# Two attention blocks on one core: V loads ahead of a K wave that has an x transfer behind it, and the second batch's x transposed one step later

## The chip, the core and the metric

The kernel runs on one core of a Trainium2 chip. Its time is the device time of one execution in microseconds, and the median over a few executions is compared. A profile is one more execution, recorded by the hardware profiler; its own time is given beside it. The core has a matrix engine (TensorE, "PE" in the profile, with its weight loads as "PEld"), three engines for elementwise work (VectorE "DVE", ScalarE "ACT", GpSimd "POOL"), a sequencer that issues most DMA transfers (SyncE, "SP") and 16 DMA engines that carry them out. TensorE writes to PSUM banks; the other engines copy from there to SBUF.

## What is computed

Two attention blocks of the same shape (A and B) run after each other, and their outputs stand side by side. For each of 16 batches and 16 heads, with 144 queries, 512 cached keys and a head size of 256:

```python
q = (x @ wq).reshape(B, Sq, H, Dh).transpose(0, 2, 1, 3)
scores = jnp.einsum("bhqd,bhkd->bhqk", q, k_cache) * (Dh ** -0.5)
p = softmax(scores, axis=-1)
o = jnp.einsum("bhqk,bhkd->bhqd", p, v_cache)
return o.transpose(0, 2, 1, 3).reshape(B, Sq, H * Dh) @ wo
```

x is 16 x 144 x 448, the caches are 16 x 16 x 512 x 256, wq is 448 x 4096 and wo 4096 x 448, all in bfloat16. The caches are most of what has to be read.

## The kernel before

**Units and steps.** A unit is one head of one batch of one block; there are NT = 512 of them. The program is a long list of steps i from -4 (`s_min = -LT`) on, and in step i it does, for TensorE in this order: a transpose of K for unit i+4 (only for the first P0 = 48 units, `t_tr`), the query projection of a later unit (`t_q`, "Q", three or four units ahead; from the 49th unit on mostly two batches in one, so that some steps have none), the scores of unit i+2 or i+3 (`t_s`, "S"), the product with V of unit i (`t_pv`, "PV"), the row sums (`t_sum`) and pieces of the output projection (`t_op_piece`). The exponentials and the logarithm are on ScalarE, most copies out of PSUM on VectorE, the partial row sums on GpSimd. A scheduler records every instruction with what it reads and writes and puts in the waits. Each engine runs its list in order, so an instruction that waits holds up everything behind it on its engine.

**Loads.** All big loads go through SyncE's queue, in one order:
- V: `t_load_v(G)` brings V for the two units 2G and 2G+1 (512 KB) into one of NV = 9 slots of `v_sb`. It is needed at PV of unit 2G. In this text v181 is the load for units 362 and 363.
- K: the first 48 units' K is loaded as it lies (`t_load_n`, "n", into the same slots) and transposed by TensorE. After that a K wave, `t_load_k(W)`, brings 16 units (two first waves 8) by one DMA transpose into `kt_sb`, which holds KR = 32 units. A wave overwrites what the wave before the last brought, so it has to wait for the last S on that. k21 is the wave for units 368 to 383.
- x: batches 0 and 1 of block A are loaded as they lie (`t_load_xn`) and transposed by TensorE in the steps that X_AT names (`t_tr_x`, L1018, with copies at L1024 on VectorE and L1028 on ScalarE). The other batches come in groups (X_GROUPS, mostly four batches) by DMA transposes (`t_load_x`, L982 to L990) into NX = 6 places. x6 is the group with batches 24 to 27 (8 to 11 of block B).
- wq and wo by plain loads in groups (`t_load_wq`, `t_load_wo`); the first two heads' wq go through ScalarE's queue.

**The planner.** The order of the loads is worked out when the program is built. `clock` sums assumed durations of TensorE work for each step, and `at(i)` is when step i begins by it. Each load has a due time (`at` of its first use, minus MARGIN = 1.0), a step from which its place is free, and an assumed duration: 1.44 for a V, 2.0+0.55 for each batch of an x group, 2.4+0.97 for each unit of a K wave. `slip` is how far the plan has fallen behind so far. From these the loop takes one load after the other. Among loads that can start now it takes the one with the smallest latest start (due time plus slip minus duration). Between a K wave and another load the rule is another one: the K wave goes first if the other's latest start is later than the wave's duration plus HOLD from now:

```python
if k_new == k_old:
    better = latest < best[1]
elif k_new:
    better = best[1] > start + m[2] + HOLD
else:
    better = latest <= start + best[2][2] + HOLD
```

Right after a K wave an x group that can start goes first, and counts 1.4 less. The first four loads are fixed by the list `first` (x of batch 0, two halves of K, x of batch 1). `dma_plan` is then issued in this order; each load's semaphores make SyncE wait until its place is free.

**The start.** Before the first data arrive TensorE runs WARM = 34 matmuls on ones (L930). Step -4 transposes x of batch 0, step -3 x of batch 1 and then does Q of unit 0 (batch 0), step -2 does Q of unit 1 (batch 1).

Of the kernel before, what the change touches and what calls it, by code (L numbers as in the profile page):

```python
# [752 lines left out]
def bass_concat_heads__mha_block_cached__gqa_block_cached__near_ridge_kernel(  # L753
# [45 lines left out]
    X_GROUPS = ((2, 6), (6, 10), (10, 14), (14, 18), (18, 20), (20, 24), (24, 28), (28, 32))  # L799
    assert X_GROUPS[-1][1] == NP * Bn and H == KW  # L800
    WQ_GROUPS = ((2, 4), (4, 8), (8, 12), (12, 16))
    WARM = 34
    NQT, NPT, NPS, NRI, NOST = 11, 4, 2, 2, 2
    RS = 3
    RC = RS * 128
    XR, X_AT = 48, {0: -4, 1: -3}
    OP_DELAY, OP_START, OP_RATE = 2, (28, 16), ((240, 1.0), (292, 1.35), (600, 1.15))
    MARGIN, HOLD, K_FIX = 1.0, 1.0, 2.4
    NXGT = len(X_GROUPS)

    P0 = NNAT * UV
# [11 lines left out]
    with contextlib.ExitStack() as es:  # L823
# [79 lines left out]
        def t_init():  # L903
# [23 lines left out]
            def e6(t):  # L927
                ins = None
                for _ in range(WARM):
                    ins = t.matmul(op_ps[:, 0:128], lhsT=ones[:, :], rhs=ones[:, :], start=True, stop=True)  # L930
# [439 lines left out]
        s_min = -LT  # L1370
# [59 lines left out]
        def at(i):  # L1430
            return clock[max(i, s_min)]
# [14 lines left out]
        def load_list():  # L1446
            made = []

            def load(use, free, took, fn, *args):
                made.append((at(use) - MARGIN, free, took, fn, args))  # L1450

            for XG, (g0, g1) in enumerate(X_GROUPS):
                load(first_q[g0], (g1 - NX) * H - lq(NT) if g1 > NX else s_min, 2.0 + 0.55 * (g1 - g0), t_load_x, XG)
            for W, (u0, u1) in enumerate(WAVES):
                last = u1 - 1 - KR
                load(u0 - ls(u0), last - ls(last) + 1 if last >= 0 else s_min, K_FIX + 0.97 * (u1 - u0), t_load_k, W)
            for pr in range(NP):
                for h0, h1 in WQ_GROUPS if pr == 0 else [(h, h + 4) for h in range(0, H, 4)]:
                    load(first_h[pr, h0], NU - H + h1 - lq(NU) if pr else s_min, 0.78 * (h1 - h0), t_load_wq, pr, h0, h1)
                for wg in range(NWG):  # L1460
                    load(wo_use[pr, wg], wo_done[pr - 1, wg] + 1 if pr else s_min, 1.3, t_load_wo, pr, wg)
            for g in X_AT:
                load(X_AT[g], s_min, 0.4, t_load_xn, g)
            for u in range(4):
                load(u - LT, s_min, 0.72, t_load_n, u // 2, u % 2)
            for G in range(2, NNAT):
                load(UV * G - LT, None, 1.44, t_load_n, G)
            for G in range(NT // UV):
                load(UV * G, None, 1.44, t_load_v, G)
            return made  # L1470

        todo = sorted(load_list(), key=lambda m: m[0])
        dma_plan, due, ring_free, now, slip = [], [], [], 2.0, 0.0
# [3 lines left out]
        while todo:  # L1477
            n = len(ring_free)
            v_lo = ring_free[n - NV] if n >= NV else s_min
            best = None  # L1480
            after_k = len(dma_plan) and dma_plan[-1][0] is t_load_k
            for m in todo[:60]:
                lo = v_lo if m[1] is None else m[1]
                start = max(now, at(lo) + slip if lo > s_min else now)
                latest = m[0] + slip - m[2]
                if len(first) and m[3:] == first[0]:
                    best = (start, -1e9, m, lo)
                    break
                if after_k and m[3] is t_load_x and start <= now:
                    best = (start, latest, m, lo)  # L1490
                    break
                if best is None or max(start, now) < max(best[0], now):
                    best = (start, latest, m, lo)
                elif max(start, now) == max(best[0], now):
                    k_new, k_old = m[3] is t_load_k, best[2][3] is t_load_k
                    if k_new == k_old:
                        better = latest < best[1]
                    elif k_new:
                        better = best[1] > start + m[2] + HOLD
                    else:  # L1500
                        better = latest <= start + best[2][2] + HOLD
                    if better:
                        best = (start, latest, m, lo)
            if first:
                first.pop(0)
            now, _latest, m, lo = best
            now += m[2] - (1.4 if after_k and m[3] in (t_load_k, t_load_x) else 0.0)
            slip = max(slip, now - m[0])
            todo.remove(m)
            dma_plan.append(m[3:])  # L1510
            due.append(lo)
            if m[1] is None:
                v_seq["n" if m[3] is t_load_n else "v", m[4][0]] = len(ring_free)
                ring_free.append(UV * (m[4][0] + 1) - (LT if m[3] is t_load_n else 0))
# [141 lines left out]
```

## Time and profile before

| | us |
|---|---|
| median of 4 runs | 1053.46 |
| lowest and highest | 1051.64, 1055.43 |
| profiled execution: its time | 1055.05 |
| profiled execution: span from first to last instruction | 1053.3 |
| TensorE waits over 1 us with work of the kernel behind them | 4.0 (V), 3.1 (V), 2.0 (K wave), 1.4 (x of batch 1) |
| K wave by DMA transpose, median from issue to landing | 24.1 (A), 24.9 (B) |
| V load, median from issue to landing | 7.2 (A), 7.6 (B) |

The profile's page gives the busy time of each engine, the waits of an engine give who was waited for (total, times, longest), a timeline gives start, duration, engine, line and operation in order of time, with a wait in brackets. "SPq" rows are DMA issues on SyncE; their duration is that of the issue, and the landing of the data is later. The windows view gives for chosen stretches the busy time of each engine, the clock that TensorE was granted (1.00 is full) and the DMA engines' share.

### The profile page before, as it was taken

How to read it: one execution, taken by the hardware profiler on the slowest of the kernel's cores; microseconds unless marked ns; L12 is line 12 of the kernel's file. 1: busy time of each engine (PE TensorE's matmuls, PEld its weight loads, DVE VectorE, ACT ScalarE, POOL GpSimd, SP SyncE). 2: the span in 40 equal slices, each digit the busy share in tenths (PEclk: the TensorE clock that was granted, in tenths of full speed). 3: DMA queues.
4: the chain of work that ended last, by engine and by line, in shares of the span. 5: the costliest groups of instructions: out<-in, count | busy, mean ns of one | idle time of the engine just before them, and what ended most of it. 6: DMA issues, size and time to landing. Idle time of an engine off the chain costs nothing.

```text
span 1053.3 us, 32452 instructions
## 1 busy us (share of the span) xinstructions
PE 1034.5 (98%) x12434; PEld 878.7 (83%) x12434; DVE 740.0 (70%) x2042; ACT 794.1 (75%) x2368; POOL 635.0 (60%) x1030
## 2 busy tenths in 40 slices
PE   9999999999998999999999999999899999999997
PEld 8999888888886888888888788888788888888885
DVE  5776677777665776777776677777576667777775
ACT  6877677777775787777867678787687777788785
POOL 3655556666664666666655566666565656666673
PEclk9999999999999999999999999999999999999999
DMA  9999999999999999999999999999999999999950
GB/s 328 366 333 322 298 260 255 278 279 285 293 281 302 274 253 272 279 291 298 270 295 353 254 282 290 291 285 292 287 283 246 296 251 311 281 272 285 283 200 13
DMA packets 590884, 294.10 MB, mean 279 GB/s; under 512 B 501440, under 2 KB 515904, under 8 KB 590720
## 3 DMA queue, kind: packets, MB, share of 16 engines
q1 hardware_dynamic: 589760, 291.49, 110.9%
q8 instruction: 99, 1.62, 0.6%
q10 hardware_dynamic: 960, 0.46, 0.2%
q14 instruction: 65, 0.53, 0.1%
HBM read 161.74 MB, written 4.13 MB: 157 GB/s over the span
## 4 chain that ended last, share of the span: by engine, by line
PE 93%; DMA 4%; ACT 1%; SPq 1%; DVE 1%; issue 0%; POOL 0%; ACTq 0%; DVEq 0%
PE s_ps L1164 23%; PE ot_ps L1220 23%; PE qp_ps L1133 23%; PE op_ps L1336 19%; DMA kt_sb<-in_B_k_cache_dram 2%; PE ot_ps L1236 2%; PE s_ps L1084 1%; PE qp_ps L1084 1%; PE qp_ps L1336 1%; DMA v_sb<-in_A_v_cache_dram 1%; ACT rinv_sb L1257 0%; DMA wo_sb<-in_A_x_dram 0%; DMA v_sb<-in_B_v_cache_dram 0%; ACT pt_sb L1174 0%; SPq L982 0%
## 5 line engine op out<-in xcount | busy, mean ns | idle before, releaser
L1184 POOL TENSOR_TENSOR pp_sb<-pt_sb 128x288 f32<-128x288 bf16 x512 | 384.2, 750 | 321.7 <-ACT pt_sb L1174 307.1
L1174 ACT ACTIVATE pt_sb<-s_ps 128x288 bf16<-128x288 f32 x1024 | 364.5, 408 | 175.9 <-PE s_ps L1164 169.6
L1272 DVE TENSOR_TENSOR ring<-ot_ps,rinv_sb 128x288 bf16<-128x288 f32 (+2 forms) x640 | 241.6, 394 | 150.9 <-ACT rinv_sb L1257 147.4
L1220 PE MATMUL ot_ps<-pt_sb,v_sb 128*128 128x144 bf16 x4096 | 340.7, 226 | 7.1 <-DMA v_sb<-in_A_v_cache_dram 4.0
L1164 PE MATMUL s_ps<-qt_sb,kt_sb 128*128 128x144 bf16 x4096 | 340.6, 226 | 2.9 <-DMA kt_sb<-in_B_k_cache_dram 2.0
L1164 PEld LDWEIGHTS s_ps<-qt_sb,kt_sb 128*128 128x128 bf16 x4096 | 287.5, 98 | 56.1 <-DVE qt_sb L1147 5.6
L1257 ACT ACTIVATE rinv_sb<-ln_sb 64x144 f32<-64x144 f32 x928 | 298.3, 321 | 24.2
L1133 PE MATMUL qp_ps<-xt_sb,wq_sb 128*128 128x288 bf16 (+1 forms) x2368 | 302.0, 271 | 0.3 <-DVE qt_sb L1146 0.2
L1336 PE MATMUL op_ps<-wo_sb,ring 128*128 128x448 bf16 x1120 | 286.3, 353 | 0.0
L1220 PEld LDWEIGHTS ot_ps<-pt_sb,v_sb 128*128 128x128 bf16 x4096 | 274.5, 98 | 8.3 <-DMA v_sb<-in_A_v_cache_dram 4.2
L1133 PEld LDWEIGHTS qp_ps<-xt_sb,wq_sb 128*128 128x128 bf16 x2368 | 212.0, 98 | 75.2 <-DVE qt_sb L1146 0.9
L1189 POOL TENSOR_TENSOR p_sb<-pp_sb 128x144 f32<-128x144 f32 x464 | 226.7, 489 | 74.7 <-DVE ps_sb L1198 10.1
L1287 DVE TENSOR_REDUCE run_sb<-ot_ps 128x1 bf16<-128x144 f32 x560 | 146.4, 304 | 83.4 <-ACT ln_sb L1244 52.6
L1198 DVE TENSOR_TENSOR ps_sb<-p_sb 64x144 bf16<-64x144 f32 x464 | 158.3, 341 | 45.8 <-POOL p_sb L1189 32.4
L1147 DVE CAST qt_sb<-qp_ps 128x576 bf16<-128x576 f32 x216 | 162.0, 750 | 16.2 <-PE qp_ps L1133 13.9
L1336 PEld LDWEIGHTS op_ps<-wo_sb,ring 128*128 128x128 bf16 x1120 | 93.9, 98 | 20.1
L1244 ACT ACTIVATE ln_sb<-ot_ps 128x144 f32<-128x144 f32 x232 | 67.7, 292 | 40.3 <-PE ot_ps L1236 33.4
L1236 PE MATMUL ot_ps<-ps_sb,ones 128*128 128x144 bf16 x280 | 63.5, 227 | 0.0
L1146 DVE CAST qt_sb<-qp_ps 128x288 bf16<-128x288 f32 x80 | 35.8, 447 | 2.2 <-PE qp_ps L1133 1.8
L1092 ACT ACTIVATE kt_sb<-qp_ps 128x512 bf16<-128x512 bf16 x48 | 29.0, 604 | 1.2 <-PE qp_ps L1084 1.2
L1189 POOL TENSOR_TENSOR ps_sb<-pp_sb 128x144 bf16<-128x144 f32 x48 | 23.4, 488 | 6.9 <-PE ot_ps L1236 0.3
L1236 PEld LDWEIGHTS ot_ps<-ps_sb,ones 128*128 128x128 bf16 x280 | 27.5, 98 | 0.0
(37 smaller groups left out, 163.8 us busy)
## 6 DMA issues: line engine op xcount, KB each, us to landing
v_sb<-in_A_v_cache_dram SPq DMA_DIRECT2D x128, 512.0 KB, 7.2
v_sb<-in_B_v_cache_dram SPq DMA_DIRECT2D x128, 512.0 KB, 7.6
v_sb<-in_A_k_cache_dram SPq DMA_DIRECT2D x22, 512.0 KB, 9.7
out_dram<-ost_sb SPq DMA_DIRECT2D x36, 112.0 KB, 6.3
wo_sb<-in_A_wo_dram SPq DMA_DIRECT2D x8, 448.0 KB, 8.0
wo_sb<-in_B_wo_dram SPq DMA_DIRECT2D x8, 448.0 KB, 8.3
wq_sb<-in_B_wq_dram SPq DMA_DIRECT2D x4, 768.0 KB, 9.7
wq_sb<-in_A_wq_dram SPq DMA_DIRECT2D x3, 768.0 KB, 9.2
```

The source lines that it names most:

```text
L1133: ins = t.matmul(acc, lhsT=wq_sb[:, kc, c0:c0 + 128], rhs=xt_sb[:, kc, xo:xe + 1:max(xe - xo, 1), :], start=(kc == 0), stop=(kc == 3))
L1147: return v.tensor_copy(qt_sb[:, a:b + 1:b - a, :, :], qp_ps[:, :, 0:2 * SQ].rearrange("p e (u q) -> p u e q", u=2))
L1164: ins = t.matmul(s_ps[bank][:, (c % 2) * SQ:(c % 2 + 1) * SQ], lhsT=kt_sb[:, 2 * c + dc, ko:ko + 128], rhs=qt_sb[:, qsl, dc, :], start=(dc ...
L1174: return a.activation(pt_sb[:, psl, 2 * k:2 * k + 2, :].rearrange("p b q -> p (b q)"), s_ps[bank][:, 0:2 * SQ], AF.Exp, scale=DH ** -0.5)
L1184: return g.tensor_tensor(pp_sb[:, :, :], pt_sb[:, psl, 0:2, :], pt_sb[:, psl, 2:4, :], op=ALU.add)
L1189: return g.tensor_tensor(dst, pp_sb[:, 0, :], pp_sb[:, 1, :], op=ALU.add)
L1198: return v.tensor_tensor(ps_sb[p0:p0 + 64, sl, :], p2_sb[0:64, :], p2_sb[64:128, :], op=ALU.add)
L1220: ins = t.matmul(ot_ps[ob][:, dc * SQ:(dc + 1) * SQ], lhsT=v_sb[:, vsl, j, c * DH + dc * 128:c * DH + (dc + 1) * 128], rhs=pt_sb[:, sl, c, ...
L1257: return a.activation(rinv_sb[p0:p0 + 64, sl, :], ln_sb[h0:h0 + 64, :], AF.Exp, scale=-1.0)
L1272: ins = v.tensor_tensor(ring[:, 2 * h:2 * h + 2, r0:r0 + q1 - q0], ot_ps[ob][:, 0:2 * SQ].rearrange("p (c q) -> p c q", c=2)[:, :, q0:q1], ...
L1287: return v.tensor_reduce(run_sb[:, k, j:j + 1], ot_ps[ob][:, 2 * SQ:3 * SQ], axis=AX.X, op=op)
L1336: ins = t.matmul(acc[0:m, 0:D], lhsT=ring[:, c, col0:col0 + m], rhs=wo_sb[:, c, :], start=(c == op_first), stop=(c == op_last))
```

## The change

Three constants and the planner's rule are changed. WARM goes from 34 to 32. X_AT has x of batch 1 transposed in step -2, ahead of that step's K transpose and of Q of unit 1, instead of in step -3. And where the planner weighs a K wave against another load, the bound is raised by the durations of all x groups (times X_HOLD = 1.0) whose place is free at that moment:

```diff
-    WARM = 34
+    WARM = 32
...
-    XR, X_AT = 48, {0: -4, 1: -3}
+    XR, X_AT = 48, {0: -4, 1: -2}
...
-    MARGIN, HOLD, K_FIX = 1.0, 1.0, 2.4
+    MARGIN, HOLD, K_FIX, X_HOLD = 1.0, 1.0, 2.4, 1.0
...
             after_k = len(dma_plan) and dma_plan[-1][0] is t_load_k
+            behind = sum(X_HOLD * m[2] for m in todo[:60] if m[3] is t_load_x and (m[1] == s_min or at(m[1]) + slip <= now))
             for m in todo[:60]:
...
                     elif k_new:
-                        better = best[1] > start + m[2] + HOLD
+                        better = best[1] > start + m[2] + HOLD + behind
                     else:
-                        better = latest <= start + best[2][2] + HOLD
+                        better = latest <= start + best[2][2] + HOLD + behind
```

No load, no compute instruction and no buffer is added or removed apart from the two matmuls on ones; what changes is the order of loads on SyncE's queue and of TensorE's work in steps -3 and -2.

## The prediction

> **What bounds the kernel now.** I read the page's busy shares first, then who TensorE waited for, then the SyncE timeline around the waits, then the granted clock in the windows beside them.
>
> ```profile
> PE 1034.5 (98%) x12434; PEld 878.7 (83%) x12434; DVE 740.0 (70%) x2042; ACT 794.1 (75%) x2368; POOL 635.0 (60%) x1030
> DMA  9999999999999999999999999999999999999950
> ```
>
> TensorE is busy 98% of the span, and the DMA engines are as full. So TensorE sets the end, and what is to be won lies in the few waits that it has:
>
> ```profile
> PE ot_ps L1220 <- DMA v_sb<-in_A_v_cache_dram: 4.0, 1, 4.0
> PE ot_ps L1220 <- DMA v_sb<-in_B_v_cache_dram: 3.1, 1, 3.1
> PE s_ps L1164 <- DMA kt_sb<-in_B_k_cache_dram: 2.0, 1, 2.0
> PE op_ps L1018 <- DMA wo_sb<-in_A_x_dram: 1.4, 1, 1.4
> ```
>
> Two waits for V, one for a K wave, one for the second batch's x at the start. Each is a single event. The SyncE timeline at the second one:
>
> ```profile
> 722.68 1.65 SPq L1054 DMA_DIRECT2D v_sb<-in_B_v_cache_dram  x3
> 725.77 22.39 SPq L1040 DMA_TRANSPOSE kt_sb<-in_B_k_cache_dram  x1
> 748.20 3.33 SPq L982 DMA_TRANSPOSE xt_sb<-in_B_x_dram  x1
> 751.58 2.63 SPq L1054 DMA_DIRECT2D v_sb<-in_B_v_cache_dram  x5
> ```
>
> The last V before the wave is v180, the wave is k21 (wave 21), then x6, then v181. v181 landed at 755.40 (3.8 after its issue), and PV of unit 362 waited for it until 755.53. After a long wait the clock is lost too:
>
> ```profile
> 4.10:7.51 3.41, 1.97 (x40) 1.61 (x37) 0.75 (x2) 0.77 (x2) 0.00 (x0) 1.00 1.07 307
> 7.51:10.93 3.42, 3.42 (x33) 3.34 (x33) 1.69 (x4) 0.88 (x2) 0.00 (x0) 0.50 1.05 382
> 598.01:601.43 3.42, 2.44 (x27) 1.72 (x24) 2.20 (x7) 1.64 (x5) 1.32 (x3) 1.00 1.29 257
> 601.43:604.84 3.41, 2.43 (x28) 2.08 (x29) 0.63 (x2) 1.35 (x4) 1.05 (x2) 1.00 1.16 272
> 751.62:755.03 3.41, 0.81 (x11) 0.57 (x9) 1.43 (x3) 0.80 (x3) 1.96 (x4) 1.00 1.14 300
> 755.03:758.45 3.42, 2.92 (x21) 2.50 (x22) 1.05 (x4) 1.34 (x4) 0.00 (x0) 0.50 1.04 362
> ```
>
> The second column is the stretch's length, the third PE's busy time, the third from the end the granted clock. A stretch with 1.44 us idle (1.97 busy) is followed by one at half clock, one with 0.98 idle (2.44 busy) is not.
>
> **The start: WARM and X_AT.** WARM drops two matmuls of 3.50/34 = 0.10 us each. That is 0.2 us if nothing covered it; it is covered, since the next PE work waits for loads whose issue doesn't move: 0. X_AT adds and removes nothing: 12 transposes, a 0.38 us DVE copy and a 0.28 us ACT copy go behind the rest of step -3 (TR of unit 1, Q of unit 0). The x load keeps its place, because the list `first` fixes it, and no queue is passed. PE then does TR1 and Q0 while the x is on its way (landed 6.95), so the 1.4 us wait and the half-clock stretch behind it go. I place TX1 at 7.08 as before, TR2 at 7.9 (its K half, issued 2.81, landed 5.0 later), Q1 at 8.45 (behind the x copies, now directly ahead of it), TR3 at 9.7 instead of 11.58: 1.9 earlier. But this runs into loads that don't move. v1 landed at 16.8 (issue 6.75 plus 10.1) and PV2 would be there at 18.50-1.9 = 16.6. The second wq group landed at 22.7 (issue 9.07 plus 13.6); Q of unit 8, which needs it, ran at 23.30 and can't be ahead of 22.8. Of 1.9 us at most 0.5 stays. The new wait before Q8 is about 1.1 us, between 0.98 (no half clock) and 1.44 (half clock, half of 3.41 us = 1.7 lost). So the start is worth -0.5 to +1.2; I take -0.3.
>
> By the Trainium skill (TensorE: Matmul & The Clock Gate, section on the HAM clock gate) the array goes back to half rate only after at least one idle window of some 3.4 us. The trace differs: 1.44 us idle inside 3.41 was enough. By the page no new wait of 1 to 2 us would have a clock price, and the upper ends here would be 1.2 to 1.7 lower; the rows decide.
>
> **The planner.** Its numbers only order loads; they are no times of the chip. Each load has a latest start: due time plus slip minus its duration. A K wave (17.92) is taken ahead of the best other load if that one's latest start is more than 17.92+HOLD = 18.92 away. The change adds 4.2 for a four-batch x that could start now. Worked through the kernel before, K and x are ready together in two decisions alone. At k7 the best other load has 23.77, and the new bound is 23.12: k7 still goes first. So the 4.0 us wait (v76, behind the next wave, k8, with no x near) is not touched. At k16 (the 2.0 us wait) x5 is 14.3 short of ready, at k2 x1 14.6 short: not touched. At k21 v181 has 19.66: above 18.92, below 23.12. There the order changes: v181, x6 (20.73 against v182's 22.04), v182, and k21 since v183 then has 20.22 and no x is behind. Carried on: k22 after v189 (v190 has 18.97 against 18.92, a close one), k23 after v196, k24 after v203 instead of v205. From x7 on the order is the old one. What is queued behind k24 on SyncE is v204, and PV408 waits for it.
>
> **The price in the middle.** Gone: PV362 is due at 748.47+3.80 = 752.27 and ran at 755.53 (3.26). The next pair has no Q, so it should take 3.80-0.98 = 2.82 and took 4.21: 1.39 of half clock. Together 4.65, the most that this part can give. Against it stands the DMA chain, which was full from v180's landing (733.90) to v206's (848.60). Before, PV408 ran at 847.23 with v204 long there; now v204 is behind k24. I add landing to landing, from the nearest rows: v181 1.35; x6 behind a V 2.7 (0.94 for the half-size x4 behind a V, 1.84 for x6 behind a K, 3.70 for x0 behind a wo load; I go between the latter two since a K right behind an x was 0.5 to 2 cheaper and v182 now parts them); v182 1.3; k21 17.7 (17.0 to 17.8); v183 1.9 (1.2 to 2.0 behind a K); six more V's and a store 10.1; k22 17.3 (15.6 to 17.8); v190 1.9; six and a store 9.5; k23 17.6 (17.3 to 18.9); v197 1.9; six and a store 9.4; k24 17.5; v204 1.9 (1.2 to 2.4). The sum is 112.05, so v204 lands at 845.95. Without new waits PV408 would be at 847.23-4.65 = 842.58, so 3.4 us come back as waits of some 1.7 (v190), 0.4 (v197) and 1.3 (v204), and 847.23-845.95 = 1.3 stays. All lower ends (0.5 for x6) give 837.8: no wait, 4.65 gained. All upper ends give 849.7: 2.4 lost. After PV412 V's slack was 7.7 us before, so nothing more is given back.
>
> **Sum.** -1.3 and -0.3 are -1.6 us on the profiled execution: 1055.05 (span 1053.3 and 1.75 around it) becomes 1053.4. The median of the runs shown lies 1.6 below the profiled one; I move it alike: 1053.46 to **1051.9**.
>
> **Rivals.**
> 1. *No new wait.* For it: k21 to k23 each left V's of slack behind them (v189 1.7, v196 0.7 us) and DMA time may be saved where k22 and k23 are issued earlier. Against: seven V's between waves where the old order had up to ten. Then 4.65+0.3: 1048.5.
> 2. *k24 in front of v204 costs more than v181 did.* Place: PV408. It decides from v204's landing after 847.23, with a half-clock stretch (1.4) behind a wait over some 1.4 us. For it: the old order had ten V's ahead of k24 and 7.7 us of slack, the new one seven. Against: two V's less in the chain up to there. At the upper ends 2.4+1.4-0.3 = 3.5 lost: 1057.0; halfway 1055.2.
> 3. *It doesn't do what it says:* the wait moves one for one from v181 to v190, or the close decision at k22 falls the other way and the plan slides back into the old one. 1053.2.
>
> **Chances.** Forecast 0.45, rival 1 0.30, rival 2 0.15, rival 3 0.10. A measurement of this kernel tells from no change what is over 0.3%, 3.2 us. Faster: rival 1 and a little of the forecast's tail, 0.33. Slower: the upper part of rival 2, 0.09. Within: 0.58. The likeliest case's own range is 1050.3 to 1053.3; with the others, 2 in 10 left out, 1048.4 to 1055.4.
>
> **What would show it.** Right: the SyncE timeline has the x transposes ahead of the K wave at about 725 and two V's around them; no V wait at 752; the 4.0 and 2.0 us waits stand; the first x wait is gone and a wait for wq of about 1 us stands at 22; V waits of 1 to 2 us at about 787 and 845. Wrong: no wait at 845 (then rival 1), one over 3 us there (rival 2), or another order in the first batch of waves, which would make the planner's arithmetic wrong; x6 landing over 4 us behind v181 would make the chain wrong.

## The result, and the profile after

| | before | changed |
|---|---|---|
| median of all comparison runs, us | 1054.68 (78 runs) | 1052.30 (52 runs) |
| lowest and highest | 1048.82, 1059.33 | 1046.93, 1057.94 |
| profiled execution: time and span | 1055.05, 1053.3 | 1051.89, 1050.0 |

The ratio is 0.9978, 95% interval 0.9969 to 0.9987: 2.3 us less, 1.4 to 3.3 by the interval. The predicted 1051.9 is 0.4 below the median. That closeness is partly luck: the forecast took 1.6 us off a median of 1053.46 from four runs, and over 78 runs the kernel before has 1054.68. The forecast gain of 1.6 lies inside the measured interval, 0.7 below its middle. One execution differs from the next by a standard deviation of 2.4 us, so a single profile shows where time goes in that execution, and not how much the change is worth.

The page's busy rows, beside those shown of before:

```profile
PE 1036.5 (99%) x12432; PEld 880.3 (84%) x12432; DVE 741.1 (71%) x2042; ACT 794.7 (76%) x2368; POOL 636.6 (61%) x1030
DMA  9999999999999999999999999999999999999950
```

TensorE and the DMA engines are as full as before. The waits of TensorE (total, times, longest):

```profile
PE s_ps L1164 <- DMA kt_sb<-in_B_k_cache_dram: 3.3, 1, 3.3
PE ot_ps L1220 <- DMA v_sb<-in_A_v_cache_dram: 1.9, 1, 1.9
...
PE ot_ps L1220 <- DMA v_sb<-in_B_v_cache_dram: 0.4, 1, 0.4
...
PE qp_ps L1133 <- ACT xt_sb L1028: 0.3, 1, 0.3
```

The 3.1 us wait for a V of block B is gone, and so is the 1.4 us wait for the second batch's x (0.3 us for its copy is left). But the wait for wave k16 has grown from 2.0 to 3.3, and the one for v76 has shrunk from 4.0 to 1.9. SyncE around the changed place:

```profile
722.21 1.97 SPq L1054 DMA_DIRECT2D v_sb<-in_B_v_cache_dram  x4
724.87 9.77 SPq L982 DMA_TRANSPOSE xt_sb<-in_B_x_dram  x1
734.68 0.58 SPq L1054 DMA_DIRECT2D v_sb<-in_B_v_cache_dram  x1
735.31 19.31 SPq L1040 DMA_TRANSPOSE kt_sb<-in_B_k_cache_dram  x1
754.66 1.61 SPq L1054 DMA_DIRECT2D v_sb<-in_B_v_cache_dram  x3
```

Four V's up to v181, x6, v182, then k21: the predicted order, and it goes on as predicted to k24 (ahead of v204) and x7. Behind x7 it is not quite the old one, as the prediction had it: k26 now goes ahead of v221, where it went ahead of v223 before, and the room of v221 (from its landing to its use) falls from 20.1 to 2.0 us. No wait came of it in this execution. The windows view (length, then busy time of PE, PEld, DVE, ACT and POOL, granted clock, DMA share, GB/s), at the start, at v76, at k16 and at the place of the change:

```profile
10.16:13.57 3.41, 3.41 (x31) 3.41 (x30) 0.94 (x3) 1.42 (x3) 0.85 (x2) 1.00 1.08 345
13.57:16.98 3.41, 3.41 (x58) 3.41 (x57) 1.35 (x4) 2.60 (x8) 2.23 (x4) 1.00 1.05 386
...
327.60:331.01 3.41, 1.50 (x16) 1.03 (x15) 0.97 (x3) 1.35 (x4) 2.44 (x4) 1.00 1.05 391
331.01:334.43 3.42, 3.42 (x42) 2.86 (x40) 1.95 (x5) 2.18 (x7) 0.51 (x1) 1.00 1.05 388
597.25:600.66 3.41, 1.17 (x11) 0.55 (x8) 1.74 (x6) 1.29 (x5) 1.22 (x2) 1.00 1.30 256
600.66:604.08 3.42, 2.39 (x18) 2.19 (x19) 0.10 (x1) 1.46 (x4) 0.73 (x1) 0.50 1.07 238
604.08:607.49 3.41, 3.41 (x21) 2.44 (x20) 1.34 (x3) 0.47 (x2) 0.49 (x1) 0.50 0.95 303
751.05:754.46 3.41, 3.41 (x42) 2.85 (x40) 2.35 (x7) 2.61 (x9) 2.50 (x4) 1.00 1.25 133
754.46:757.88 3.42, 3.42 (x47) 2.96 (x45) 2.33 (x7) 3.11 (x11) 2.00 (x3) 1.00 1.09 271
```

The execution before, at v76:

```profile
328.40:331.78 3.38, 0.11 (x2) 0.12 (x3) 0.00 (x0) 0.00 (x0) 1.04 (x2) 1.00 0.97 303
331.78:335.19 3.41, 3.41 (x19) 2.31 (x18) 0.98 (x3) 0.93 (x3) 0.00 (x0) 0.50 1.01 378
```

At 751 to 758 TensorE is busy throughout at full clock; that is the gain. At 597 to 607 there are two half-clock stretches that the execution before didn't have. At the start the record of the clock begins only at 13.57 us (up to there the view prints 1.00 for want of a record): 31 matmuls in the stretch before it, 58 in the one behind it.

Starts of PV of chosen units, taken from the traces (us from the span's start), show where the profiled 3.2 us come from:

| | PV8 | PV150 | PV154 | PV268 | PV288 | PV360 | PV364 | PV408 | PV511 |
|---|---|---|---|---|---|---|---|---|---|
| before | 30.55 | 323.31 | 337.14 | 564.54 | 609.44 | 748.47 | 759.74 | 847.23 | 1042.86 |
| changed | 31.90 | 324.50 | 334.56 | 562.50 | 611.52 | 750.43 | 757.05 | 844.56 | 1040.20 |
| difference | +1.35 | +1.19 | -2.58 | -2.04 | +2.08 | +1.96 | -2.69 | -2.67 | -2.66 |

The middle (PV360 to PV364) gave 4.65, all that it could. The v76 wait gave 3.8 by another landing and no half clock behind it; the start took 1.35, and k16 took 4.1 (1.3 of wait, 2.8 of half clock). Neither v76 nor k16 was moved in the order of the loads. So the profiled 3.2 is not the middle's gain alone: the other three terms, 3.8 won and 1.35 and 4.1 lost, took 1.7 of the 4.65 back in this execution. The 0.5 us still missing to the profiled 3.2 lie behind the last PV and around the span.

### The profile page after: what moved, and what is told of

It reads as the page before. It is cut to its first block, busy times and chain, and to the rows that moved or that the text cites. A ratio compares the mean times of both kernels' runs of the same rounds, so it can differ in the third digit from the quotient of the medians.

```text
span 1050.0 us, 32447 instructions
## 1 busy us (share of the span) xinstructions
PE 1036.5 (99%) x12432; PEld 880.3 (84%) x12432; DVE 741.1 (71%) x2042; ACT 794.7 (76%) x2368; POOL 636.6 (61%) x1030
## 4 chain that ended last, share of the span: by engine, by line
PE 94%; DMA 3%; ACT 1%; DVE 1%; SPq 0%; issue 0%; POOL 0%; ACTq 0%; DVEq 0%; POOLq 0%
PE s_ps L1164 24%; PE ot_ps L1220 23%; PE qp_ps L1133 23%; PE op_ps L1336 19%; DMA kt_sb<-in_B_k_cache_dram 2%; PE ot_ps L1236 2%; PE s_ps L1084 1%; PE qp_ps L1084 1%; PE qp_ps L1336 1%; DMA v_sb<-in_A_v_cache_dram 0%; DMA v_sb<-in_B_v_cache_dram 0%; ACT rinv_sb L1257 0%; ACT pt_sb L1174 0%; PE op_ps L930 0%; SPq L1054 0%
## 5 line engine op out<-in xcount | busy, mean ns | idle before, releaser
L1147 DVE CAST qt_sb<-qp_ps 128x576 bf16<-128x576 f32 x216 | 162.0, 750 | 16.9 <-PE qp_ps L1133 14.5
L1336 PEld LDWEIGHTS op_ps<-wo_sb,ring 128*128 128x128 bf16 x1120 | 93.8, 98 | 20.1
```

Source lines behind the costliest of these rows:

```text
L1147: return v.tensor_copy(qt_sb[:, a:b + 1:b - a, :, :], qp_ps[:, :, 0:2 * SQ].rearrange("p e (u q) -> p u e q", u=2))
L1336: ins = t.matmul(acc[0:m, 0:D], lhsT=ring[:, c, col0:col0 + m], rhs=wo_sb[:, c, :], start=(c == op_first), stop=(c == op_last))
```

## The experiments

**Theory A**, formed from this table: k16's landing is set by DMA work alone, so nothing before unit 288 counts. Its rivals: **B**, the new start costs; **C**, the new start is part of the gain; later **L**, each wait counts by itself, **T**, TensorE sets the end and the waits are accidents, and **D**, which took A's place. Each run is compared with the kernel before on the same chip: e1 to e4 on one chip, e5 to e11 on a second, e12 on a third. The last column is the ratio less one, times the median of the kernel before. The ratio is estimated for itself and is not the quotient of the two medians: e9's medians differ by 4.6 us, where its ratio says 7.0.

| run | median, us | kernel before, us | ratio (95%) | us against before |
|---|---|---|---|---|
| e1 rule only | 1053.65 | 1055.85 | 0.9973 (0.9953 to 0.9992) | -2.9 |
| e2 start only | 1054.65 | 1055.85 | 0.9993 (0.9974 to 1.0013) | -0.7 |
| e3 late start | 1055.17 | 1055.85 | 0.9997 (0.9978 to 1.0017) | -0.3 |
| e4 k16 early | 1055.21 | 1055.85 | 0.9987 (0.9965 to 1.0009) | -1.4 |
| e5 X_HOLD 1.2 | 1050.36 | 1056.48 | 0.9950 (0.9931 to 0.9970) | -5.3 |
| e6 small wo | 1049.67 | 1056.48 | 0.9931 (0.9907 to 0.9955) | -7.3 |
| e7 k22 to k24 later | 1051.80 | 1056.48 | 0.9959 (0.9939 to 0.9979) | -4.3 |
| e8 HOLD 2.0 | 1052.40 | 1056.48 | 0.9965 (0.9943 to 0.9987) | -3.7 |
| e9 e5 and k22 to k26 later | 1051.76 | 1056.38 | 0.9934 (0.9908 to 0.9961) | -7.0 |
| e10 changed kernel again | 1052.22 | 1056.38 | 0.9956 (0.9933 to 0.9979) | -4.6 |
| e11 e9 with the old start | 1052.90 | 1056.38 | 0.9963 (0.9938 to 0.9988) | -3.9 |
| e12 e5, k22 to k24 later, WARM 44 | 1051.20 | 1056.19 | 0.9958 (0.9944 to 0.9971) | -4.4 |

An interval is 3 to 6 us wide, so the traces have to tell most of it. From each profiled execution (us; "239 done" is the end of S of unit 239, "S288" the start of the scores that need k16):

| | PV8 | 239 done | S288 | PV360 | 360 to 364 | 364 to 408 |
|---|---|---|---|---|---|---|
| before | 30.55 | 497.57 | 602.41 | 748.47 | 11.27 | 87.49 |
| e2 | 32.38 | 500.41 | 606.17 | 752.34 | 13.22 | 87.48 |
| changed | 31.90 | 495.01 | 601.69 | 750.43 | 6.62 | 87.51 |
| e10 | 30.36 | 491.76 | 602.71 | 750.31 | 6.62 | 87.67 |
| e3 | 30.91 | 496.25 | 599.58 | 750.14 | 6.62 | 87.55 |
| e1 | 30.69 | 498.67 | 603.69 | 751.25 | 6.62 | 88.86 |
| e4 | 30.33 | 493.86 | 599.72 | 750.03 | 6.62 | 90.47 |
| e5 | 30.16 | 491.87 | 598.24 | 744.45 | 6.62 | 90.79 |
| e6 | 29.91 | 497.50 | 600.51 | 746.45 | 6.62 | 89.78 |
| e8 | 31.76 | 492.52 | 599.90 | 747.51 | 6.61 | 88.44 |
| e7 | 30.08 | 491.11 | 597.17 | 744.77 | 6.61 | 87.57 |
| e9 | 32.44 | 494.06 | 604.49 | 752.09 | 6.62 | 87.71 |
| e11 | 30.47 | 491.41 | 597.53 | 745.12 | 6.62 | 87.51 |
| e12 | 30.41 | 491.47 | 602.87 | 751.62 | 6.62 | 87.51 |

PV408 to PV511 took 195.6 to 195.7 in all but e7 (196.7, with waits at v214 and v221).

### e1 and e2: the rule alone, the start alone

```diff
e1, against the changed kernel
-    WARM = 32
+    WARM = 34
-    XR, X_AT = 48, {0: -4, 1: -2}
+    XR, X_AT = 48, {0: -4, 1: -3}
e2, against the kernel before
-    WARM = 34
+    WARM = 32
-    XR, X_AT = 48, {0: -4, 1: -3}
+    XR, X_AT = 48, {0: -4, 1: -2}
```

> Theory A (a barrier): the landing of wave k16 near 602 us is set by DMA work alone, so whatever TensorE gains or loses before unit 288 ends as a longer or shorter wait there; the rule's gain at PV362 (4.65 us in the profiled execution before) lies behind it and counts in full. Then the rule alone is worth what the whole change is: 2.4 us below the kernel before on the median, within 0.8, with no V wait near 752 and the x wait at the start still there. Theory B (the start gives part back): the new start costs about 2 us, so the rule alone is 3.5 to 4.7 us below the kernel before. Theory C (the start brings part of it): the rule alone is only 0.5 to 1.5 us below.

> Only WARM and X_AT of the change, the order of the loads as before. Theory A: within 0.5 us of the kernel before; the x wait of 1.4 us is gone, v181 is still waited for (about 3 us), and what PV2 to PV100 gain in time is gone again at unit 288. Theory B: 1 to 2.3 us slower than before. Theory C: 1 to 2 us faster.

The waits of e1, then of e2:

```profile
PE ot_ps L1220 <- DMA v_sb<-in_A_v_cache_dram: 3.9, 1, 3.9
PE s_ps L1164 <- DMA kt_sb<-in_B_k_cache_dram: 2.1, 1, 2.1
PE ot_ps L1220 <- DMA v_sb<-in_B_v_cache_dram: 1.2, 1, 1.2
PE op_ps L1018 <- DMA wo_sb<-in_A_x_dram: 1.2, 1, 1.2
```

```profile
PE ot_ps L1220 <- DMA v_sb<-in_A_v_cache_dram: 4.7, 1, 4.7
PE ot_ps L1220 <- DMA v_sb<-in_B_v_cache_dram: 4.0, 1, 4.0
PE s_ps L1164 <- DMA kt_sb<-in_B_k_cache_dram: 2.9, 1, 2.9
```

The rule alone is worth 2.9 us (0.8 to 5.0), which is what the whole change is worth; the start alone 0.7 (from 2.7 faster to 1.4 slower), not told from nothing. So, as far as these two tell, the gain is the rule's; B at its full 2 us lies outside e2's interval, a smaller start effect of either sign is not excluded. In e2 the wait for v181 is still there (4.0 us, and 360 to 364 takes 13.2), in e1 it is gone, and 1.2 us stand in its place for a V of block B: v204, at PV408 (846.68 landed, 846.73 used). That is one of the waits that the prediction expected and the profile of the changed kernel didn't show.

### e3 and e4: theory A's own tests

```diff
e3, against the changed kernel
-    WARM = 32
+    WARM = 60
e4, against the changed kernel, behind the planner's loop
+        j = next(k for k, (fn, args) in enumerate(dma_plan) if fn is t_load_k and args[0] == 16)
+        for lst in (dma_plan, due):
+            lst.insert(j - 1, lst.pop(j))
```

> The changed kernel with 60 instead of 32 matmuls on ones, so that the first transposes begin later (28 matmuls at 0.05 to 0.10 us each are 1.4 to 2.9 us, of which the first loads' arrival hides some). Theory A: the delay is swallowed by the waits for v76 near 331 us and k16 near 602 us, which get shorter by it: the time stays within 0.5 us of the changed kernel (2.4 below the kernel before), and PV288 runs at the same time as before to within 1 us. Theories B and C, by which the start counts to the end: 1 to 2.7 us slower than the changed kernel, about the time of the kernel before.

> The changed kernel with wave k16 issued one place earlier, ahead of v143 (22 us of slack in the profile of the changed kernel) instead of behind it; nothing else moves. Theory A: k16 lands one V earlier (1.2 to 1.4 us), the 3.3 us wait for it becomes 1.9 to 2.1, and with it, where the wait no longer costs a half-clock stretch (1.7 us each), more is won: 1.2 to 3 us below the changed kernel, 3.5 to 5.5 below the kernel before. If instead TensorE sets the end there (B, C), nothing: within 0.5 us of the changed kernel. A loss would mean that v143 lands too late for PV286 (it has some 1 us of room).

e3's time is 0.3 below the kernel before (from 2.3 below to 1.8 above), where A wanted 2.4 below, just outside. Its trace contradicts A more clearly: PV288 ran 2.8 us before the kernel before's, as k16 landed at 599.44. This lead was gone at PV340 (1.7 behind): a wait of 2.8 us for v166 at 694 and a half-clock stretch. In e4 k16 landed 81.4 us after k14, against 81.9 in the changed kernel, 0.5 less and not 1.2 to 1.4. With the V still in front of it e3 had 81.0 and e8 82.7, so one profile doesn't show what the V is worth there. Behind it v144 (0.13 us of room), k17 (0.13) and v190 and v197 (0.05 and 0.13) ran out of room. The time is 1.4 below the kernel before (from 3.7 below to 1.0 above), where A wanted 3.5 to 5.5; the low end of that is not excluded by the time. By their traces both were misses for A as stated: loads run out of room at several places and not at k16 alone.

### e5 and e6: a wait taken away ahead of k14, DMA work taken away behind it

```diff
e5, against the changed kernel
-    MARGIN, HOLD, K_FIX, X_HOLD = 1.0, 1.0, 2.4, 1.0
+    MARGIN, HOLD, K_FIX, X_HOLD = 1.0, 1.0, 2.4, 1.2
e6, against the changed kernel, in t_load_wo
-                return q.dma_start(wo_sb[:, c0:c0 + WOG, :],
-                                   w[c0 * 128:(c0 + WOG) * 128, :].rearrange("(c p) n -> p c n", p=128)).then_inc(
+                src = w[c0 * 128:(c0 + WOG) * 128, :].rearrange("(c p) n -> p c n", p=128)
+                rows = 16 if pr else 128
+                return q.dma_start(wo_sb[0:rows, c0:c0 + WOG, :], src[0:rows]).then_inc(
```

> The changed kernel with X_HOLD 1.2: k7's bound becomes 23.96, above v70's 23.77, so that x2 goes ahead of k7 and v76 ahead of k8; from k11 on the order is that of the changed kernel. The 1.9 to 4.0 us wait for v76 goes. Theory A (from about k14 to v204 the DMA chain sets the end): TensorE is 2 to 4 us earlier from PV154 to PV284, waits that much longer for k16, and PV360 and the time are the changed kernel's to within 1 us (the half clock behind a longer wait may cost up to 3.4 us). Theory L (each wait counts by itself): 2 to 5.7 us below the changed kernel.

> The changed kernel with only 16 of the 128 partitions of block B's wo loaded (the rest keeps block A's rows, so block B's output projection is computed with other numbers): 8 loads of 1.3 us each become some 0.2 us, 8 to 9 us of DMA work less between k15 and k16, and TensorE's work the same. Theory A: k16 lands at about 593 instead of 601.6, no wait for it and no half clock behind it, the waits at v190, v197 and v204 have 4 us and more of room: PV288 at about 599 (2.5 before the kernel before, without the half clock 6 before), the time 4 to 8 us below the changed kernel. Theory T (TensorE sets the end and the waits seen are accidents of single executions): within 1 us.

SyncE in e5 between k7 and k8, and the waits of e5:

```profile
296.12 1.81 SPq L1054 DMA_DIRECT2D v_sb<-in_A_v_cache_dram  x2
297.98 0.47 SPq L1365 DMA_DIRECT2D out_dram<-ost_sb  x1
298.49 2.62 SPq L1054 DMA_DIRECT2D v_sb<-in_A_v_cache_dram  x5
303.88 20.75 SPq L1040 DMA_TRANSPOSE kt_sb<-in_A_k_cache_dram  x1
```

```profile
PE s_ps L1164 <- DMA kt_sb<-in_B_k_cache_dram: 3.7, 2, 3.3
PE ot_ps L1220 <- DMA v_sb<-in_B_v_cache_dram: 2.3, 3, 1.7
```

Seven V's (v70 to v76) now go ahead of k8, and no wait for a V of block A is left. PV154 ran at 331.44, 3.1 before the changed kernel's. Unlike what A says, this was not lost at k16: S288 came 3.5 before the changed kernel's, PV360 6.0 before. But then k21 (0.14 us of room), v183, v190 (0.05 each) and v197 (0.14) came too late, and 364 to 408 took 90.79: 3.3 of the lead went there. The median is 5.3 below the kernel before (3.2 to 7.3). Against the changed kernel on the same chip (e10, 4.6 below) that is 0.7, which these intervals can't tell from nothing; by the medians alone L is not shown against A.

e6 took DMA work away between k15 and k16. It leaves 112 of the 128 rows of each piece of block B's wo unloaded, so block B's output is another one, and it is no version to use. The waits:

```profile
PE ot_ps L1221 <- DMA v_sb<-in_A_v_cache_dram: 3.6, 1, 3.6
PE ot_ps L1221 <- DMA v_sb<-in_B_v_cache_dram: 2.1, 1, 2.1
```

k16 landed 77.0 us after k14 (81.0 to 85.7 in the other thirteen profiles), with 1.5 us of room, and the wait for it is gone from the view. The wait for a V of block B stands at v197, where the expectation had 4 us and more of room. Less of the DMA work was saved than expected (5 us, not 8 to 9), and the time is 7.3 below the kernel before (4.8 to 9.8). T, by which nothing should have changed, expected the changed kernel's time; e6's interval lies below the changed kernel's first one (1.4 to 3.3 below) and overlaps that of e10, so the times alone leave T standing. The trace does not: with less DMA work in front of it k16 came earlier than in any other profile, and nobody waited for it.

### e7 and e8: more V's ahead of the waves

```diff
e7, against the changed kernel, behind the planner's loop
+        for w in (22, 23, 24):
+            j = next(k for k, (fn, args) in enumerate(dma_plan) if fn is t_load_k and args[0] == w)
+            for lst in (dma_plan, due):
+                lst.insert(j + 1, lst.pop(j))
e8, against the changed kernel
-    MARGIN, HOLD, K_FIX, X_HOLD = 1.0, 1.0, 2.4, 1.0
+    MARGIN, HOLD, K_FIX, X_HOLD = 1.0, 2.0, 2.4, 1.0
```

> The changed kernel with k22, k23 and k24 each one place later, behind v190, v197 and v204. These three V's had 0.0 to 1.9 us of room in the four profiles with the new order, and two of them waited (1.2 us at v204; 2.6 at v190 and v197); the waves have 2.8, 7 and 12 us. Theory A with the give-back of the prediction: no V wait between 780 and 850, the V's next behind the waves (v191, v198, v205) with 1 to 3 us of room, the waves with 1 to 10; PV408 minus PV364 is 87.2 to 87.6 as in the executions without a wait, not 88.9 or 90.5: 0 to 3 us below the changed kernel, about 1 on the median. If the chain itself is what holds TensorE, new waits of the same size stand at v191, v198, v205 or at k22, and the time is the changed kernel's.

> The changed kernel with HOLD 2.0 instead of 1.0 (X_HOLD 1.0): x2 ahead of k7 as in the run with X_HOLD 1.2, and besides one V more ahead of k4, k8, k17, k22 and k26. Theory A: the v76 wait is gone and that is swallowed at k16; k17 lands 1.35 us later where it had 0.6 to 3.4 us of room, v151 no longer behind it, v190 no longer behind k22: within 1 us of the changed kernel. Theory L: 2 to 6 us below it.

SyncE in e7, with k22 at 755.92 and k23 at 785.40:

```profile
755.92 24.75 SPq L1040 DMA_TRANSPOSE kt_sb<-in_B_k_cache_dram  x1
780.72 1.61 SPq L1054 DMA_DIRECT2D v_sb<-in_B_v_cache_dram  x3
782.37 0.47 SPq L1365 DMA_DIRECT2D out_dram<-ost_sb  x1
782.88 2.48 SPq L1054 DMA_DIRECT2D v_sb<-in_B_v_cache_dram  x4
785.40 23.71 SPq L1040 DMA_TRANSPOSE kt_sb<-in_B_k_cache_dram  x1
```

With seven V's between the waves as before but one V later in the row, 364 to 408 took 87.57, although TensorE came to PV364 at 751.38, as early as in e5, where it took 90.79. v190, v197 and v204 had 17 us of room; v198 had 0.37 and v205 0.29, and the lead was lost in part further on, at v214 and v221 (1.1 us). So the give-back can be ordered away up to v205; e9, e11 and e12, with the same edit, took 87.5 to 87.7 there. The medians of e7 and e8 lie 4.3 and 3.7 below the kernel before, e10 on the same chip 4.6: no gain over the changed kernel is shown.

### e9 to e12: together, and the start once more

e9 is e5's edit and e7's for waves 22 to 26; e10 is the changed kernel; e11 is e9 with the old start:

```diff
e9, against the changed kernel
-    MARGIN, HOLD, K_FIX, X_HOLD = 1.0, 1.0, 2.4, 1.0
+    MARGIN, HOLD, K_FIX, X_HOLD = 1.0, 1.0, 2.4, 1.2
+        for w in (22, 23, 24, 25, 26):
...
e11, against e9
-    WARM = 32
+    WARM = 34
-    XR, X_AT = 48, {0: -4, 1: -2}
+    XR, X_AT = 48, {0: -4, 1: -3}
e12, against e9
-    WARM = 32
+    WARM = 44
-        for w in (22, 23, 24, 25, 26):
+        for w in (22, 23, 24):
```

> The changed kernel with X_HOLD 1.2 (v76 ahead of k8) and each of k22 to k26 one place later (behind v190, v197, v204, v214, v221). Theory D (it takes the place of A): k14 is issued when TensorE has done S of unit 239, and from k14's landing to v204's the DMA chain took 324.3 to 325.5 us in five of the six profiles with the new order and all its loads; so time won before unit 239 counts to the end (against A), and time won between unit 240 and PV408 only until the chain's end. The v76 wait's removal then counts: S of unit 239 ends at 491 to 492 instead of 495 to 497.6. With V's ahead of the waves PV408 comes 347 to 348.5 us after it (347.85 where k22 to k24 were later, 350.0 with X_HOLD 1.2 alone): 6.5 to 9 us below the kernel before. Theory A: only the later waves' part, 3 to 5 below it.

> The changed kernel once more, to have it on the chip of the other two. 2.4 us below the kernel before by the runs so far. Theory D: S of unit 239 ends at 494 to 498 by whether the v76 wait draws a half-clock stretch, k14 lands 22 to 24.7 later, v204 324 to 326 after that, and PV408 follows within 1 us; where TensorE is there first, V waits at v190, v197 or v204 of 0.5 to 2 us in all.

> The first kernel of these three with WARM 34 and X_AT of the kernel before. In the profiles so far PV8 ran at 30.6 and 30.7 with the old start; with the new one at 29.9 to 30.3 in four executions and at 31.8 to 32.4 in three, in which TensorE was granted the full clock for good only from 13.3 us or later. Theory D, by which the start counts to the end: the median is within 1 us of the kernel with the new start, and its profile has PV8 at 30.6 to 30.8 if the full clock stands by 6.5 us. If the new start were worth as much as the rest (theory C), 2 us slower.

> X_HOLD 1.2, k22 to k24 one place later, x of batch 1 in step -2, and 44 matmuls on ones instead of 32. The granted clock changes in stretches of 3.41 us whose phase differs from execution to execution. Where the new start with 32 went badly (PV8 at 31.8 to 32.4, four of nine profiles) the full clock stood for good only from 13.3 us or later. If too short a warm-up is the cause, 12 matmuls more (some 1 us) give the full clock by 7 us and PV8 at 30.2 to 31.0; if the waits behind the warm-up are, PV8 can come at 31.8 to 32.4 all the same. Time by theory D: 5 to 8 us below the kernel before, as with 32; the warm-up is worth at most 0.6 of it on the median, less than the runs can tell.

All four lie 3.9 to 7.0 below the kernel before, and no two of them are told apart. A version that beats the changed kernel is not shown, though e9 has the lowest ratio with all loads. e11, with the old start, is 3.1 us behind e9 by the ratios and 1.1 by the medians; the intervals overlap, so this pair doesn't say what the start is worth. e12's 4.4 missed the 5 to 8 that D expected.

Theory D is, by these profiles, at most half right. Its first half, that time won before unit 239 counts: the six profiles with 239 done by 492.5 have S288 at 599.7 in the mean (597.2 to 602.9), the four with it at 496 to 501 and all loads at 603.0 (599.6 to 606.2). Of 6.5 us of lead at unit 239 (491.7 against 498.2) 3.2 are left. The two groups overlap and differ in their load orders, so this is a trend and no measure. The expected constant, k14's landing to v204's, held at 324 to 326 in five profiles and was 328 in e4 and e10; and in e9, e10 and e12 S288 came 110 to 111 us after unit 239 instead of 103 to 107 (there v134 was waited for, 2.3 to 2.5 us, and k16 landed 84.4 to 85.7 us after k14 instead of 81.0 to 82.7). What slows the loads there in some executions is open. e9's PV408 came 352.4 after unit 239, not 347 to 348.5; e11's 347.85.

The start: with the new one and 32 matmuls PV8 ran at 29.9 to 30.4 in five profiles and at 31.8 to 32.4 in four (30.9 with WARM 60), with the old one at 30.5 to 30.7 in three. In the four late ones the full clock stood for good from 13.3 to 14.5 us, in the five from 4.4 to 6.1. Of the four, two (changed, e8) have no full clock on record before that, and two (e2, e9) had it from 4.1 or 4.3 to 7.5 or 7.7 us and lost it behind 1.48 and 1.56 us idle. e12, with 44 matmuls, had it from 4.57 and PV8 at 30.41; one execution doesn't show that the longer warm-up does it.

## Why the prediction came out, point by point

**The order of the loads** was right in every place up to x7, the close decision at k22 included; "it doesn't do what it says" is out. Behind x7 the prediction expected the old order, and k26 went two V's earlier, which cost nothing in the profile (PV408 to PV511 took 195.6 before and after).

**What goes at PV362** was right to 0.01 us: 3.26 of wait and 1.39 of half clock, 4.65 in the profile. It is there in all twelve profiles with the new order: 360 to 364 takes 6.62. In e2, with the old order, it takes 13.22, so the old wait cost some executions more than the profile of before showed.

**What comes back** (3.4 us at v190, v197 and v204) is the term that was mis-sized for the profiled execution: it came back as 0. The places were right: v190, v197 and v204 have the least room of the V's around them (1.36, 0.92 and 0.58 us). The sum's landing of v204 was 845.95, the profile has 843.98: the chain began 0.6 earlier (v180 landed at 733.32) and took 110.7 us, not 112.05. And TensorE reached PV360 at 750.43, 2 us later than the sum had it, owing to k16. These two, 2.0 us each, are more than the 3.4.

What decides is how far ahead of TensorE the chain is. From v182's landing to v204's the chain took 103.8 to 106.4 us in the eight profiles with k24 directly ahead of v204, and TensorE takes 94.1 from PV360 to PV408 without a wait, so v182 has to land some 10 to 12 us ahead of PV360. By the prediction's terms it was 9.2. Ordered by that distance, 364 to 408 lost, over 87.5: changed 11.6 us, 0.0; e8 (one V more ahead of k22) 11.0, 0.9; e10 10.8, 0.2; e3 10.7, 0.0; e6 10.4, 2.3; e1 10.1, 1.4; e4 9.9, 3.0; e5 7.4, 3.3. At 9.2 the row has about 3, near the predicted 3.4.

So rival 1 (no new wait) is the profiled execution, and the forecast is what the altered kernels e4, e5 and e6 come near to (2.3 to 3.3). The load order of the changed kernel itself was profiled four times (changed, e10, and e1 and e3 with another start) and lost 0.0, 0.2, 1.4 and 0.0, so 3.4 was too much for it, and of the 4.65 some 3.3 to 4.65 stay there. The rule alone moved the time 2.9, the whole change 2.3; where the rest goes is not shown. Rival 2's place was real (v204 waited for in e1), but no wait there came to its price: nothing over 1.2 at PV408.

**The start** was put at -0.3, with -0.5 and +1.2 as ends. The x wait went, and the wait for the second wq group came in some executions (0.9 us in e4 and e10, 0.3 in e5) and not in the profiled one, which ran late enough. At PV8 the nine profiles of the new start with 32 matmuls stand 0.7 before to 1.9 behind the 30.6 of the old: the upper end was too low, because the prediction let the half-clock stretch go with the wait. It went in five of nine; in four TensorE ran at half clock longer than before.

**The 4.0 and 2.0 us waits** should have stood. They moved without their loads being moved: v76's was 1.9, 3.9, 4.7, 2.7, 2.1 and 3.6 us in runs with the same order there, and 0.1 in two (e7, e10). The prediction took each for a fixed size.

**The sum** added start and middle. By the trend above about half of a lead at unit 239 is gone by unit 288, and what is left shortens the chain's lead at PV360 and can come back behind it, so the terms do not simply add. That was not measured for the start itself. It did little harm because the start's term was small.

**The clock.** The prediction weighed a row of 1.44 us idle followed by half clock against the Trainium skill (TensorE: Matmul & The Clock Gate, section on the HAM clock gate), by which the rate falls only after an idle window of some 3.4 us. The row's limit fell: 1.91 us idle at v76 in the changed kernel, and 1.70 and 1.63 in two neighbouring stretches of e5 (below), were followed by full clock. The page's rule taken word for word does not hold either: 2.24 idle in 3.41 was followed by half clock.

All fourteen profiles, counted from 20 us on in stretches of 3.41 us from where the clock's record begins, put a limit to it. The clock fell eighteen times, each time behind a stretch with 1.97 us or more idle, and never behind one with 1.91 or less. The smallest, in e4:

```profile
632.75:636.16 3.41, 1.44 (x20) 1.16 (x19) 1.61 (x5) 0.72 (x3) 0.76 (x2) 1.00 1.11 291
636.16:639.58 3.42, 3.42 (x24) 2.59 (x22) 1.03 (x4) 2.04 (x7) 2.25 (x4) 0.50 1.01 371
```

How long it stayed down goes with the half-clock stretch itself: with 0.90 us or more idle in it a second one followed (six times), with 0.50 or less it did not (twelve times).

## What to carry to other kernels

Where TensorE and the DMA engines are both full, a wait that is removed was, in this kernel, worth its length only up to the room of the next loads in the queue: tabulate landing and use of each load behind it, as that distance decides what is left of the wait. Look at several executions of the same program before giving a wait a size, and put loads with little room ahead of those with much (a V with 1 us ahead of a wave with 8) before making anything faster. In e7 that order took the waits at v190, v197 and v204 away; a gain on the median is not shown for it. An edit that lets TensorE arrive earlier at a load that lands when it lands can cost more clock than it wins time: the changed kernel was 2.0 us ahead at PV268 and 2.1 behind at PV288.

## What the runs showed that was not expected

A wait of 3.3 us cost no clock in e5 and two half-clock stretches in the changed kernel, at the same load. The stretches of 3.41 us lie differently in each execution. e5's wait fell across two of them:

```profile
593.19:596.61 3.42, 1.72 (x20) 1.09 (x17) 2.28 (x6) 1.65 (x5) 1.22 (x2) 1.00 1.27 258
596.61:600.02 3.41, 1.78 (x22) 1.56 (x23) 0.00 (x0) 1.29 (x4) 0.55 (x1) 1.00 1.18 250
```

Neither had over 1.7 us idle, and the clock stayed. In the changed kernel one stretch took 2.24 us of it (1.17 busy), over the limit, and the next two ran at half clock; the first of these had 1.03 us idle, as in the other five such pairs it had 0.90 or more. Behind the warm-up less was enough: 1.61 us idle in e11 (1.80 busy from 3.75 to 7.16) was followed by half clock, and 1.35 in e1 (2.06 busy from 6.32 to 9.73) was not.

A K wave of 16 units landed 22.1 to 25.8 us after its issue at the same place (k14).
